# Joined feature sums and a split accumulator bank in the first stage of an attention and mixture kernel

## The chip, the cores and the metric

The kernel runs on one core of one Trainium2 chip. The metric is the device time of one execution in microseconds. The core has TensorE (PE, matrix products; its weight loads are shown as PEld), VectorE (DVE), ScalarE (ACT), GpSimd (POOL) and SyncE (SP, which issues nearly all transfers). TensorE writes its products into accumulator banks, and VectorE and ScalarE read them from there.

## The reference

Three layers follow each other, all in float32. The first is a linear attention with exponential features of both signs:

```python
def phi(x):
    proj = np.einsum('bhsd,df->bhsf', x, w_phi)
    proj = proj - np.max(np.abs(proj), axis=-1, keepdims=True)
    return np.concatenate([np.exp(proj), np.exp(-proj)], axis=-1)
q_p, k_p = (phi(q), phi(k))
kv = np.einsum('bhsf,bhsd->bhfd', k_p, v)
z = np.sum(k_p, axis=2)
num = np.einsum('bhsf,bhfd->bhsd', q_p, kv)
den = np.einsum('bhsf,bhf->bhs', q_p, z)[..., None] + 1e-06
```

There are 4 sequences of 576 tokens, 8 heads of 64 and 128 features of either sign. The second layer normalises each of the 2304 tokens and applies a gated feed-forward (512 to 1536 to 512). The third is a soft mixture of 8 experts with 4 slots each: softmax over tokens into the slots, two products per expert, softmax over slots back to the tokens.

## The kernel before

The work has a first stage (keys and values), a second stage (six blocks of 384 tokens through the gated feed-forward, with the query side of later blocks between) and a last stage (the experts and the output). The change lies in the first.

The first stage goes over 18 tiles of 128 tokens. For a tile, `project` makes the key projections P (L503: sixteen instructions on 64 rows of the array by 128 columns, two products at a time), `shift` takes the largest absolute value and subtracts it on VectorE (L507, L511), `exps` makes both exponentials on ScalarE (L524, L525) into a tile `kp`. Then `kv` adds to three accumulators of the sequence. `kv_of` (L548) multiplies values (64 columns of the array at a time, two products side by side) with the features of one half of the heads, and `z_of` (L557) multiplies a column of ones (32 columns at a time, four side by side), which sums the features. In a trace one product in float32 is two instructions. A sequence ends in the middle of tiles 4 and 13, so these have two parts, and there are 20 parts in all. At the end of a sequence `Evac` copies the accumulators out and `turn` transposes them (kvt, L585).

Between these stand the steps of block 0's query side, class `Rows`: `project` (L389, P from qraw), VectorE's largest and difference (L392, L393), `turn` (L404, T) and ScalarE's exponentials (L406); later `attend` (L449, o), `scale` and `out` (L476, yT). Their place in the code comes from the table `TURNED0`.

The accumulator memory of this stage has three banks for the sums, two for P and three buffers under the tag "misc" for everything else: block 0's P and T, o, yT and kvt. `WARM` products of zeros that nobody reads run at the start while the first transfers are under way (L609).

Each engine executes its instructions in the order of its queue. That order is not the order of the code: a scheduler in the language's layer lays it out when the program is built, by dependencies and its own costs. Semaphores hold an instruction until what it needs has ended.

Of the kernel before, what the change touches and what calls it, by code (L numbers as in the profile page):

```python
# [7 lines left out]
F32 = mybir.dt.float32  # L8
F32R = mybir.dt.float32r
U32 = mybir.dt.uint32  # L10
AF = mybir.ActivationFunctionType
ALU = mybir.AluOpType
# [4 lines left out]
NB, NH, SEQ, HD, DF = 4, 8, 576, 64, 128  # L17
NT, DM, DFF = 2304, 512, 1536
NE, SPE, FE = 8, 4, 1024
NS = NE * SPE  # L20
TILES = NT // 128
BLK = 384
NBLK = NT // BLK
TPB = BLK // 128
# [4 lines left out]
KCONV, MCONV = (3, 2), (2, 2)  # L29
NX = 4  # L30
CFIRST = 7
WARM = 3
NLEFT = 2
ELEFT = 4
CTURN = 4
# [32 lines left out]
def tile_kernel(ctx: ExitStack, tc: tile.TileContext, q2T, qT, kT, v, wbd, wg, wv, wo, rmsg, phi, w1, w2, consts, out):  # L68
    nc = tc.nc
    PE, DVE, ACT, POOL, SP = nc.tensor, nc.vector, nc.scalar, nc.gpsimd, nc.sync  # L70
# [30 lines left out]
    xp = pool(qctx, "xp", side="right")  # L101
# [4 lines left out]
    ident = cst[:, 0:128]  # L106
# [85 lines left out]
    kvt = {}  # L192
    xraw = {}
# [11 lines left out]
    class Q:  # L205
# [3 lines left out]
        def __init__(self, sp, ps, blk, bufs):  # L209
            self.sp, self.ps, self.blk, self.bufs = sp, ps, blk, bufs  # L210
            self.raw, self.x, self.e = {}, {}, {}

        def psum(self, name, shape):
            return self.ps.tile(shape, F32, tag="misc", name=name, bufs=self.bufs["misc"])

        def numerator(self, c, e):
            if c == 0:
# [160 lines left out]
    class Turned(Q):  # L378
# [5 lines left out]
                SP.dma_start(out=self.raw[c], in_=q2T[self.blk, c])  # L384

        def project(self, c, i):
            p = self.psum("P", [128, 2, DF])
            o = p.rearrange("p h f -> p (h f)")
            PE.matmul(out=o, lhsT=self.raw[c][:, 128 * i:128 * i + 128], rhs=wbd_f, start=True, stop=True)  # L389
            mx = self.sp.tile([128, 2, 1], F32, tag="mx", name="qmx", bufs=2)  # L390
            self.pr = self.sp.tile([128, 2, DF], F32, tag="pr", name="qpr", bufs=self.bufs["pr"])
            DVE.tensor_reduce(out=mx, in_=p, axis=AX.X, op=ALU.max, apply_absolute_value=True)  # L392
            DVE.tensor_tensor(out=self.pr, in0=p, in1=mx.to_broadcast([128, 2, DF]), op=ALU.subtract)  # L393
            if i == TPB - 1:
                self.load(c + self.bufs["raw"])
            return self.pr

        def turn(self, c, i, pr):
            if i == 0:
                self.e2 = self.sp.tile([128, 2, 2, BLK], F32, tag="e", name="e2", bufs=self.bufs["e"])  # L400
                self.e[2 * c], self.e[2 * c + 1] = self.e2[:, 0], self.e2[:, 1]
            tp = self.psum("T", [128, 2, 128])
            for h in range(2):
                PE.transpose(out=tp[:, h], in_=pr[:, h], identity=ident)  # L404
            for s in range(2):
                ACT.activation(out=self.e2[:, :, s, 128 * i:128 * i + 128], in_=tp, func=AF.Exp, scale=1.0 - 2.0 * s)  # L406
# [30 lines left out]
    class Rows(Turned):  # L437


        def attend(self, c):  # L440
            if c == 0:
                self.y = self.sp.tile([128, TPB, 4, 2, HD], F32, tag="y", name="y", bufs=1)
            e = [self.e.pop(2 * c), self.e.pop(2 * c + 1)]
            o = self.psum("o", [128, TPB, 2, HD + 1])
            for i in range(TPB):
                for b, r0, r1 in batch_parts(self.blk * TPB + i):
                    for hh in range(2):
                        for s in range(2):
                            PE.matmul(out=o[r0:r1, i, hh], lhsT=e[hh][:, s, 128 * i + r0:128 * i + r1],  # L449
                                      rhs=kvt[b][:, 2 * c + hh, s], start=s == 0, stop=s == 1, skip_group_check=True)  # L450
            rd = self.sp.tile([128, TPB, 2, 1], F32, tag="rd", name="rd", bufs=2)
            DVE.tensor_scalar(out=rd, in0=o[:, :, :, HD:HD + 1], scalar1=1e-6, scalar2=None, op0=ALU.add)
            DVE.reciprocal(out=rd, in_=rd)
            DVE.tensor_tensor(out=self.y[:, :, c], in0=o[:, :, :, 0:HD], in1=rd.to_broadcast([128, TPB, 2, HD]), op=ALU.mult)
            for b, t0, t1 in block_parts(self.blk):
                if c == 3 and self.blk * BLK + t1 == (b + 1) * SEQ and b + 2 < NB:
                    kvt[b + 2] = kvp.tile([128, NH, 2, HD + 1], F32, tag="kv", name=f"kv{b + 2}", bufs=2)
                    SP.dma_start(out=kvt[b + 2].rearrange("p h s d -> p (h s d)"), in_=kv_d[b + 2])

        def scale(self):  # L460
            sq = self.sp.tile([128, 2, 2, BLK], F32, tag="e", name="sq", bufs=self.bufs["e"]).rearrange("p a b t -> p (a b t)")
            ms = self.sp.tile([128, TPB], F32, tag="ms", name="ms", bufs=1)
            rows = [self.y[:, i].rearrange("p c h d -> p (c h d)") for i in range(TPB)]
            for i in range(TPB):
                ACT.activation(out=sq[:, DM * i:DM * i + DM], in_=rows[i], func=AF.Square, accum_out=ms[:, i:i + 1])
            DVE.tensor_scalar(out=ms, in0=ms, scalar1=1.0 / DM, scalar2=1e-6, op0=ALU.mult, op1=ALU.add)
            rsqrt(self.sp, ms)
            for i in range(TPB):
                DVE.tensor_scalar(out=rows[i], in0=rows[i], scalar1=ms[:, i:i + 1], scalar2=None, op0=ALU.mult)

        def out(self):
            xraw[self.blk] = xp.tile([128, 4, BLK], F32, tag="xraw", name="xraw", bufs=1)
            for c in range(4):
                tp = self.psum("yT", [128, TPB, 128])
                for i in range(TPB):
                    PE.transpose(out=tp[:, i], in_=self.y[:, i, c].rearrange("p h d -> p (h d)"), identity=ident)  # L476
                ACT.activation(out=xraw[self.blk][:, c].rearrange("p (i t) -> p i t", i=TPB), in_=tp, func=AF.Copy, scale=rms_sb[:, c:c + 1])

    with ExitStack() as pk:
        kx = pool(pk, "kx")  # L480
        sp = pool(pk, "spk")
        psk = pool(pk, "psk", PSUM)
        acc = {}

        class Front:

# [30 lines left out]
        class K(Front):  # L517
# [2 lines left out]
                SP.dma_start(out=self.vt, in_=v[self.i].rearrange("p (h d) -> p h d", h=NH))  # L520

            def exps(self, hf):
                kp = sp.tile([128, 4, 2, DF], F32, tag="kp", name="kp", bufs=6)
                ACT.activation(out=kp[:, :, 0], in_=self.pr[hf], func=AF.Exp)  # L524
                ACT.activation(out=kp[:, :, 1], in_=self.pr[hf], func=AF.Exp, scale=-1.0)  # L525
                self.e[hf] = kp

            def kv(self, part):

                for f in (self.kv_of, self.z_of):  # L530
                    for hf in range(2):
                        f(hf, part)

            def ends(self, part):
                b, r0, r1 = part
# [25 lines left out]
        class Evac:  # L561
# [17 lines left out]

            def turn(self, n):  # L580
                kv = self.kv
                tp = psk.tile([128, 2, 2, 128], F32, tag="misc", name="kvt", bufs=3)
                for c in range(2):
                    for s in range(2):
                        PE.transpose(out=tp[:, c, s], in_=self.sb[n][:, c, s], identity=ident)  # L585
                for c in range(2):
                    if n < 2:
                        o = kv[:, 4 * c + n:4 * c + n + 3:2, :, 0:HD].rearrange("p h s d -> p s h d")
                        i = tp[:, c].rearrange("p s (h d) -> p s h d", h=2)
                    else:  # L590
                        o = kv[:, c::2, :, HD].rearrange("p h s -> p s h")
                        i = tp[:, c].rearrange("p s (h r) -> p s h r", h=4)[:, :, :, 0]
                    if n == 1:
                        DVE.tensor_copy(o, i)
                    else:
                        ACT.copy(out=o, in_=i)
                if n == 2 and self.b >= 2:
                    SP.dma_start(out=kv_d[self.b], in_=kv.rearrange("p h s d -> p (h s d)"))

        kb = {"tag": "k", "raw": 4, "pr": 3, "P": ("P", 2)}  # L600
        ks = [K(sp, psk, kT, i, kb if i else dict(kb, P=("misc", 3))) for i in range(TILES)]
        ks[0].load(ACT)
        SP.dma_start(out=wbd_f, in_=wbd)
        still = sp.tile([128, 256], F32, tag="kvs0", name="still", bufs=1)
# [20 lines left out]
                k.shift(hf)  # L625
                k.exps(hf)
        fillers = []
        q0 = Rows(sp, psk, 0, {"misc": 3, "raw": 2, "pr": 3, "e": 2})
        qsteps = q0.steps(TURNED0[0:4], TURNED0[4:8], TURNED0[8:])
        qsteps = [[f for m, f in qsteps if m == n] for n in range(2 * TILES)]  # L630
        q0.begin()
        for i in range(TILES):
            k, kn = ks[i], ks[i + 2] if i + 2 < TILES else None
# [85 lines left out]
    with ExitStack() as p2:  # L719
# [5 lines left out]
        sp = pool(tctx, "conv")  # L725
# [233 lines left out]
        t = gate(0, xs)  # L959
# [8 lines left out]
        for blk in range(NBLK):  # L968
            acc = [ps.tile([128, DM], F32, tag=f"acc{i}", name=f"acc{i}", bufs=1) for i in range(TPB)]
            qsteps, qnext = qnext or [], None  # L970
            if blk == 1:
                q1ctx.close()
                sp = pool(pctx, "post", side="right")
            if blk == NBLK - 1:
# [5 lines left out]
                sp = pool(pctx, "post", side="right")  # L980
                hp = pool(pctx, "hp", side="right")
            if blk:
                x2 = []
                for i in range(TPB):
                    y = sp.tile([128, DM], F32, tag="x2", name="x2", bufs=TPB)
# [27 lines left out]
            for m in range(MF):  # L1013
# [3 lines left out]
                if more:  # L1017
                    t = gate((m + 1) % MF, xs)
# [34 lines left out]
    with ExitStack() as p3:  # L1053
        sp = pool(p3, "sp3")
# [145 lines left out]
```

## Time and profile before

| | |
|---|---|
| median of 3 runs | 706.3 us (705.16 to 707.02) |
| profiled execution | 705.7 us, span 703.9 us |
| TensorE busy | 689.4 us, 98% of the span |
| VectorE, ScalarE, GpSimd busy | 468.5, 329.1, 147.2 us |
| first product of the second stage (gate of block 0) | 118.05 us from the span's start |
| transfers | 79.42 MB, mean 113 GB/s |

Times in the rows are microseconds from the start of the span unless marked ns. L12 is line 12 of the kernel before. A timeline row is a run of equal instructions of one engine; its first number is the start and its second the time that the run covers. Products overlap at their ends, so the time from one run's start to the next one's start tells more than the covered time.

### The profile page before, as it was taken

The numbers are of one execution on the slowest core, as the hardware profiler recorded it, in microseconds if no ns is written. First come the engines' busy times: TensorE is split into PE (matmuls) and PEld (weight loads), VectorE is DVE, ScalarE is ACT, GpSimd is POOL, SyncE is SP. The second block draws the span as 40 slices with busy tenths as digits, with TensorE's granted clock in tenths as the row PEclk, the third lists the DMA queues.
The fourth block names the chain that finished last, engine by engine and source line by source line (L and its number), as shares of the span: only waits on it lengthen the run. The fifth ranks groups of instructions, "written<-read, shape, count | busy, mean of one in ns | idle before, by whom it ended". The sixth has DMA issues, their size and how long they took to land.

```text
span 703.9 us, 11807 instructions
## 1 busy us (share of the span) xinstructions
PE 689.4 (98%) x4653; PEld 571.3 (81%) x4653; DVE 468.5 (67%) x915; ACT 329.1 (47%) x687; POOL 147.2 (21%) x74
## 2 busy tenths in 40 slices
PE   7999999999999999999999999999999999999995
PEld 4667766988889898998989989899897999898443
DVE  4798995888875596765857669776585753423313
ACT  4878885687745443344432554425443232112103
POOL 0000000000003355133651326523364200000100
PEclk9999999999999999999999999999999999999997
DMA  6755535434211001010000100001000085577898
GB/s 224 280 170 192 195 107 181 143 120 160 79 40 33 3 24 40 0 57 12 24 9 1 57 13 23 9 0 57 1 1 8 1 305 234 190 284 256 323 367 291
DMA packets 25143, 79.42 MB, mean 113 GB/s; under 512 B 2688, under 2 KB 13376, under 8 KB 18688
## 3 DMA queue, kind: packets, MB, share of 16 engines
q1 hardware_dynamic: 24720, 77.52, 31.4%
q10 hardware_dynamic: 368, 1.15, 0.5%
q8 instruction: 36, 0.59, 0.3%
q14 instruction: 19, 0.16, 0.1%
HBM read 71.99 MB, written 6.67 MB: 112 GB/s over the span
## 4 chain that ended last, share of the span: by engine, by line
PE 96%; DMA 1%; ACT 1%; DVE 1%; issue 0%; SPq 0%; ACTq 0%
PE pg L928 22%; PE pv L928 22%; PE acc L953 7%; PE acc L954 7%; PE acc L955 7%; PE kacc L548 5%; PE num L223 4%; PE P L503 3%; PE kacc L557 3%; PE y L1088 2%; PE y L1072 2%; PE o L449 2%; PE P L389 1%; DMA wraw<-in_wo_dram 1%; PE x2tp L738 1%; PE qP L315 1%
## 5 line engine op out<-in xcount | busy, mean ns | idle before, releaser
L928 PE MATMUL pv<-xnh,wv 128*128 128x384 f32 x576 | 117.1, 343 | 0.0
L928 PE MATMUL pg<-xnh,wg 128*128 128x384 f32 x576 | 115.1, 342 | 0.3 <-ACT xnh L121 0.3
L318 POOL PARTITION_ALL_REDUCE qe<-qe x32 | 51.9, 1634 | 297.1 <-ACT qe L317 287.9
L928 PEld LDWEIGHTS pg<-xnh,wg 128*128 128x128 f32 x576 | 102.5, 188 | 5.8 <-ACT xnh L121 0.7
L928 PEld LDWEIGHTS pv<-xnh,wv 128*128 128x128 f32 x576 | 101.7, 188 | 1.5 <-issue 1.3
L349 POOL PARTITION_ALL_REDUCE qe<-qe x32 | 82.7, 2631 | 85.8 <-DVE qe L348 56.3
L121 ACT CAST hh<-t 128x384 fp32r<-128x384 f32 x72 | 36.7, 509 | 115.2 <-PE acc L954 77.6
L953 PE MATMUL acc<-wo,hh 128*128 128x512 f32 x216 | 87.2, 404 | 0.0
L954 PE MATMUL acc<-wo,hh 128*128 128x512 f32 x216 | 86.1, 399 | 0.0
L955 PE MATMUL acc<-wo,hl 128*128 128x512 f32 x216 | 85.3, 395 | 0.0
L124 DVE TENSOR_TENSOR hl<-t,hh 128x384 fp32r<-128x384 f32 x72 | 40.1, 557 | 63.3 <-ACT hh L121 63.2
L936 DVE SCALAR_TENSOR_TENSOR t<-t,pg 128x384 f32<-128x384 f32 x72 | 39.8, 553 | 57.9 <-ACT t L935 57.7
L935 ACT ACTIVATE t<-pg 128x384 f32<-128x384 f32 x72 | 35.1, 487 | 73.1 <-PE pg L928 72.7
L928 PE MATMUL pg<-xnl,wg 128*128 128x384 f32 x288 | 65.0, 342 | 0.0
L928 PE MATMUL pv<-xnl,wv 128*128 128x384 f32 x288 | 62.4, 339 | 0.0
L940 DVE TENSOR_TENSOR t<-t,pv 128x384 f32<-128x384 f32 x72 | 39.6, 549 | 24.6 <-PE pv L928 23.6
L928 PEld LDWEIGHTS pg<-xnl,wg 128*128 128x128 f32 x288 | 51.9, 188 | 1.6 <-DVE xnl L124 0.9
L928 PEld LDWEIGHTS pv<-xnl,wv 128*128 128x128 f32 x288 | 51.7, 188 | 0.0
L955 PEld LDWEIGHTS acc<-wo,hl 128*128 128x128 f32 x216 | 40.6, 188 | 10.2 <-DVE hl L124 0.3
L953 PEld LDWEIGHTS acc<-wo,hh 128*128 128x128 f32 x216 | 40.8, 189 | 7.3 <-issue 0.3
L954 PEld LDWEIGHTS acc<-wo,hh 128*128 128x128 f32 x216 | 40.6, 188 | 6.3
L548 PE MATMUL kacc<-kp,vt 128*64 128x256 f32 (+1 forms) x320 | 41.2, 393 | 2.3 <-ACT kp L525 2.3
(207 smaller groups left out, 1051.7 us busy)
## 6 DMA issues: line engine op xcount, KB each, us to landing
eu<-in_w_dram SPq DMA_DIRECT2D x32, 1024.0 KB, 6.6
wraw<-in_wg_dram SPq DMA_DIRECT2D x6, 1024.0 KB, 4.9
wraw<-in_wv_dram SPq DMA_DIRECT2D x6, 1024.0 KB, 5.6
wraw<-in_wo_dram SPq DMA_DIRECT2D x6, 1024.0 KB, 5.5
qraw<-in_qT_dram SPq DMA_DIRECT2D x32, 192.0 KB, 2.4
vt<-in_v_dram SPq DMA_DIRECT2D x18, 256.0 KB, 3.2
out_dram<-ob SPq DMA_DIRECT2D x18, 256.0 KB, 3.0
raw<-in_kT_dram SPq DMA_DIRECT2D x17, 256.0 KB, 2.9
```

Source lines behind the costliest of these rows:

```text
L121: ACT.copy(out=hi, in_=src)
L124: (lo_eng or POOL).tensor_tensor(out=lo, in0=src, in1=hi.bitcast(F32), op=ALU.subtract)
L318: POOL.partition_all_reduce(e[:, 0], e[:, 1], channels=128, reduce_op=bass_isa.ReduceOp.absmax)
L349: POOL.partition_all_reduce(e[hh][:, 1], u, channels=128, reduce_op=bass_isa.ReduceOp.add)
L548: PE.matmul(out=kva[o0:o0 + 64, hh // 2], lhsT=self.vt[r0:r1, h], rhs=kp[r0:r1, hh].rearrange("p s f -> p (s f)"), start=first and hh < 2, ...
L928: PE.matmul(out=p, lhsT=w[:, a, c], rhs=x, start=n == 0, stop=n == 11)
L935: ACT.activation(out=t, in_=g, func=AF.Tanh, scale=0.5)
L936: DVE.scalar_tensor_tensor(out=t, in0=t, scalar=1.0, in1=g, op0=ALU.add, op1=ALU.mult)
L940: DVE.tensor_tensor(out=t, in0=t, in1=wide("v", m, xs), op=ALU.mult)
L953: PE.matmul(out=acc[i], lhsT=hh[:, s], rhs=w[:, 0], start=m == 0, stop=False)
L954: PE.matmul(out=acc[i], lhsT=hh[:, s], rhs=w[:, 1], start=False, stop=False)
L955: PE.matmul(out=acc[i], lhsT=hl[:, s], rhs=w[:, 0], start=False, stop=m == MF - 1)
```

## The change

The sums of features of a part are put off: `kv` makes the products kv at once and keeps the part in a list, and when two parts are in it, or the sequence ends, the sums of all of them are made one behind the other. For this `kp` has eight buffers in place of six. The query projections and turns of block 0 no longer take a "misc" buffer but one half of a bank of their own, each call the other half, and "misc" has two buffers in place of three. The result of `attend` goes straight into `xraw`, and `scale` and `out` work on it there, so the tile `y` is gone. There are four unread products at the start in place of three.

```diff
-WARM = 3
+WARM = 4
...
+        def half(self, name):
+
+            if "half" not in self.bufs:
+                return self.psum(name, [128, 2, 128])
+            if not self.halves:
+                t = self.ps.tile([128, 2, 2, 128], F32, tag="halves", name="halves", bufs=1)
+                self.halves = [t[:, 0], t[:, 1]]
+            self.halves.reverse()
+            return self.halves[0]
...
         def project(self, c, i):
-            p = self.psum("P", [128, 2, DF])
+            p = self.half("P")
...
-            tp = self.psum("T", [128, 2, 128])
+            tp = self.half("T")
...
-                self.y = self.sp.tile([128, TPB, 4, 2, HD], F32, tag="y", name="y", bufs=1)
+                xraw[self.blk] = xp.tile([128, 4, BLK], F32, tag="xraw", name="xraw", bufs=1)
...
-            rows = [self.y[:, i].rearrange("p c h d -> p (c h d)") for i in range(TPB)]
+            rows = [xraw[self.blk][:, :, 128 * i:128 * i + 128] for i in range(TPB)]
...
-                kp = sp.tile([128, 4, 2, DF], F32, tag="kp", name="kp", bufs=6)
+                kp = sp.tile([128, 4, 2, DF], F32, tag="kp", name="kp", bufs=8)
...
             def kv(self, part):
 
-                for f in (self.kv_of, self.z_of):
-                    for hf in range(2):
-                        f(hf, part)
+                for hf in range(2):
+                    self.kv_of(hf, part)
+                zs.append((self, part))
+                if len(zs) == 2 or self.ends(part)[1]:
+                    for k, p in zs:
+                        for hf in range(2):
+                            k.z_of(hf, p)
+                    zs.clear()
...
-                tp = psk.tile([128, 2, 2, 128], F32, tag="misc", name="kvt", bufs=3)
+                tp = psk.tile([128, 2, 2, 128], F32, tag="misc", name="kvt", bufs=2)
...
-        ks = [K(sp, psk, kT, i, kb if i else dict(kb, P=("misc", 3))) for i in range(TILES)]
+        ks = [K(sp, psk, kT, i, kb if i else dict(kb, P=("misc", 2))) for i in range(TILES)]
...
-        q0 = Rows(sp, psk, 0, {"misc": 3, "raw": 2, "pr": 3, "e": 2})
+        q0 = Rows(sp, psk, 0, {"misc": 2, "half": True, "raw": 2, "pr": 3, "e": 2})
```

Since the scheduler lays out the queues, the change also moves work that the diff does not touch. Counted in TensorE's order from the first P to the last query projection of the stage, runs of products of one kind go from 23 to 26 for kv (L548, now L563), from 21 to 13 for sums (L557, now L572) and from 17 to 25 for P (L503, now L513). Changes from one kind of product to another, where query projections, turns, kvt, o and yT count as one kind since all use the whole array, go from 76 to 92.

TensorE's order at the start, before. Idle is the unread product, P with raw the key projection, kacc with vt the products kv, kacc with small the sums; a row is a run of equal products.

```order
L609 MATMUL idle<-still 32x256 x3
L503 MATMUL P<-wbd_f,raw 128x128 x16
L548 MATMUL kacc_190<-kp,vt 64x256 x4
L557 MATMUL kacc_192<-kp,small 32x256
L548 MATMUL kacc_191<-kp,vt 64x256
L503 MATMUL P<-wbd_f,raw 128x128 x8
L548 MATMUL kacc_191<-kp,vt 64x256 x3
```

The same place of the changed kernel; halves with qraw is a query projection into the split bank.

```order
L624 MATMUL idle<-still 32x256 x4
L513 MATMUL P<-wbd_f,raw 128x128 x16
L400 MATMUL halves<-wbd_f,qraw 128x256
L563 MATMUL kacc_191<-kp,vt 64x256 x4
L563 MATMUL kacc_192<-kp,vt 64x256
L513 MATMUL P<-wbd_f,raw 128x128 x8
L563 MATMUL kacc_192<-kp,vt 64x256 x3
```

A query projection has moved ahead of the first kv, and the sums of the first part have gone from here.

TensorE's order over tiles 2 and 3, before; T with qpr is a turn of block 0's queries, P with qraw a query projection.

```order
L548 MATMUL kacc_190<-kp,vt 64x256 x4
L548 MATMUL kacc_191<-kp,vt 64x256 x4
L557 MATMUL kacc_192<-kp,small 32x256 x8
L404 MATMUL T<-cst,qpr 128x128 x2
L389 MATMUL P<-wbd_f,qraw 128x256
L404 MATMUL T<-cst,qpr 128x128 x2
L503 MATMUL P<-wbd_f,raw 128x128 x8
L548 MATMUL kacc_190<-kp,vt 64x256 x4
```

The same place of the changed kernel, with what each row waits for: DVE and Activation are VectorE's and ScalarE's semaphores, DMAHW a transfer's.

```order
L415 MATMUL halves<-cst,qpr 128x128 [waits DVE_49]
L415 MATMUL halves<-cst,qpr 128x128
L513 MATMUL P<-wbd_f,raw 128x128 [waits DMAHW6_49,DVE_49,PE_49]
L513 MATMUL P<-wbd_f,raw 128x128 x2
L513 MATMUL P<-wbd_f,raw 128x128 [waits DVE_49,PE_49]
L513 MATMUL P<-wbd_f,raw 128x128 x3
L400 MATMUL halves<-wbd_f,qraw 128x256 [waits Activation_49]
L513 MATMUL P<-wbd_f,raw 128x128
L563 MATMUL kacc_191<-kp,vt 64x256 [waits DMAHW2_49]
L563 MATMUL kacc_191<-kp,vt 64x256 x3
L563 MATMUL kacc_192<-kp,vt 64x256 x4
L572 MATMUL kacc_193<-kp,small 32x256
```

A query projection stands inside a run of key projections, seven before it and one behind; its wait is for ScalarE's exponentials of the turn ahead of it, which read the other half of the bank. The first of sixteen sums stands ahead of the next turn, and fifteen follow it.

## Rows read from the trace of the kernel before

**Rows 1.** The page, busy time with its share, and the chain of waits.

```profile
PE 689.4 (98%) x4653; PEld 571.3 (81%) x4653; DVE 468.5 (67%) x915; ACT 329.1 (47%) x687; POOL 147.2 (21%) x74
...
PE 96%; DMA 1%; ACT 1%; DVE 1%; issue 0%; SPq 0%; ACTq 0%
```

**Rows 2.** Stretches: length, each engine's busy time, granted clock (PEclk), transfer share, GB/s.

```profile
core 0: us, PE busy (x) PEld busy (x) DVE busy (x) ACT busy (x) POOL busy (x), PEclk, DMA share, GB/s
...
9.65:13.03 3.38, 3.38 (x12) 1.00 (x10) 1.59 (x3) 3.01 (x6) 0.00 (x0) 0.50 0.80 299
13.05:118.00 104.95, 103.35 (x1091) 68.49 (x1090) 89.19 (x154) 80.81 (x151) 0.00 (x0) 1.00 0.52 178
...
118.00:703.90 585.90, 576.79 (x3513) 497.94 (x3513) 373.64 (x749) 242.04 (x526) 147.02 (x70) 0.99 0.28 98
```

**Rows 3.** Timeline of TensorE, one tile: start, covered time, line, tiles, shapes, count.

```profile
26.81 1.16 PE L503 MATMUL P<-wbd_f,raw 64*128 64x128 f32 x16
27.90 1.95 PE L548 MATMUL kacc<-kp,vt 128*64 128x256 f32 x16
29.78 1.07 PE L557 MATMUL kacc<-kp,small 128*32 128x256 f32 x16
30.78 0.44 PE L404 MATMUL T<-cst,qpr 128*128 128x128 f32 x2
```

**Rows 4.** Timeline of TensorE, two shorter runs of kv.

```profile
14.31 1.08 PE L548 MATMUL kacc<-kp,vt 128*64 128x256 f32 x6
...
16.32 1.08 PE L548 MATMUL kacc<-kp,vt 128*64 128x256 f32 x8
```

**Rows 5.** Timeline of TensorE, the start; in brackets idle time and its releaser.

```profile
1.18 2.77 PE L609 MATMUL idle<-still 128*32 128x256 f32 x6 [1.18 <-DVE small L606]
4.25 2.97 PE L503 MATMUL P<-wbd_f,raw 64*128 64x128 f32 x32 [0.30 <-DMA raw<-in_kT_dram]
9.48 1.88 PE L548 MATMUL kacc<-kp,vt 128*64 128x256 f32 x8 [2.26 <-ACT kp L525]
```

**Rows 6.** The first transfer of query rows.

```profile
L384 SPq DMA_DIRECT2D qraw<-in_q2T_dram x1: 430/430/430, 5.1 to 5.1; - x1
...
DMA to landing us min/median/max: 5.4/5.4/5.4
```

**Rows 7.** Timeline of all engines around the stall at 40.84 us.

```profile
40.84 0.70 PE L389 MATMUL P<-wbd_f,qraw 128*128 128x256 f32 x2 [1.33 <-ACT kv L596]
41.07 0.41 DVE L393 TENSOR_TENSOR qpr<-P,qmx 128x256 f32<-128x256 f32 x1
```

**Rows 8.** Timeline of TensorE, query projections and turns.

```profile
38.48 0.60 PE L389 MATMUL P<-wbd_f,qraw 128*128 128x256 f32 x2
...
53.61 0.39 PE L404 MATMUL T<-cst,qpr 128*128 128x128 f32 x2
...
61.06 0.65 PE L389 MATMUL P<-wbd_f,qraw 128*128 128x256 f32 x2
61.64 1.16 PE L503 MATMUL P<-wbd_f,raw 64*128 64x128 f32 x16
...
66.31 0.38 PE L404 MATMUL T<-cst,qpr 128*128 128x128 f32 x2
```

**Rows 9.** Timeline of ScalarE, exponentials of two turns.

```profile
54.03 0.66 ACT L406 ACTIVATE e<-T 128x256 f32<-128x256 f32 x2 [0.29 <-PE T L404]
...
68.84 0.67 ACT L406 ACTIVATE e<-T 128x256 f32<-128x256 f32 x2
```

**Rows 10.** Timeline of all engines, the end of the stage.

```profile
115.78 1.53 PE L585 MATMUL kvt<-cst,kvs 128*128 128x128 f32 x12
...
116.48 0.65 ACT L596 COPY kvx<-kvt 128x256 f32<-128x256 f32 x2
...
117.35 0.24 ACT L596 COPY kvx<-kvt 128x8 f32<-128x8 f32 x2 [0.22 <-PE kvt L585]
117.47 1.35 ACT L121 CAST xnh<-xraw 128x384 fp32r<-128x384 f32 x3
...
118.05 0.62 PE L928 MATMUL pg<-xnh,wg 128*128 128x384 f32 x2 [0.30 <-ACT xnh L121]
```

## Prediction before the run

> **What bounds the kernel now.** I read three views in this order: the page's shares with its chain of waits, then busy time by stretch, then the timeline of the first stage. The page is to show that TensorE is busy for 98% of the span and makes 96% of the chain [rows 1]. By stretch, the first stage from 13.05 to 118.00 us has TensorE busy for 103.35 of 104.95 us, VectorE for 89.19 and ScalarE for 80.81 [rows 2]. So what is added to TensorE's work there moves the end by as much, and what VectorE or ScalarE gain is worth nothing unless TensorE waits for it. After 118 us TensorE is busy for 576.79 of 585.90 us in work that the change leaves alone apart from its first few products; I pass a shift of the first stage on to the end one for one.
>
> The timeline of a tile in the steady part gives the prices. From start to start the projections P take 1.09 us, the products kv 1.88, the sums of features 1.00 [rows 3]. A kv run of eight instructions takes 1.08 us and one of sixteen 1.95, so eight more cost 0.87, or 0.109 each [rows 3, 4]. Sixteen at 0.109 are 1.74: a run of kv has a fixed part of 0.14. The sums run four strips at a time, so their sixteen instructions are four rounds of 0.218 and the fixed part is 0.13. P's instructions have half the columns: 16 times 0.054 is 0.87, fixed part 0.22. A query projection of two instructions needs 0.435 and is followed by P after 0.58 [rows 8]: 0.15. On the mean a change from one kind of product to another costs 0.16 us. A second price: six kv instructions (three products) take as long as eight, both 1.08 [rows 4]. A product without a partner in the other strip costs a pair's time: 0.435 for kv, 0.22 for P.
>
> **The change part by part.** *Joined sums.* Eight pairs of runs become one run each. A saved boundary is worth 0.13: 8 x 0.13 = -1.05 us.
>
> *What the order does with the query work.* The counts of runs in TensorE's order go from 23 to 26 for kv, from 17 to 25 for P and from 76 to 92 for all changes of kind. Joining alone would have left 68, so 24 are new: projections and turns of block 0 now stand inside runs (seven P, a query projection, one P; one sum, a turn, fifteen sums). 24 x 0.16 = +3.85. Cut at odd places, five more kv products and three more P products run alone: 5 x 0.435 + 3 x 0.22 = +2.85. No other work covers this, since it is TensorE's own time in a stage in which it is the bound. From both sides: that a P run cut by a query projection pays at its exit is not in the trace, since P is followed by kv everywhere. If all the P cuts were free (8 x 2 x 0.16 and 0.65) the sum would be 3.2 less; if each cut cost twice the dearest fixed part, 24 x 0.44, it would be 6.7 more. I take 0.16, the mean of the four rows.
>
> The Trainium skill ("TensorEngine Tiling (Array Packing)", section "Key Properties") says that changing the tiling mode, not just the tile, drains the engine, and it counts row tiling as a mode. P runs in 64-row tiles and the query work on the whole array, so by that page the unseen exit is paid too and the sum keeps its 3.2; if only the width in columns counted, it would lose it. The seen prices of 0.13 to 0.22 agree with a drain.
>
> *The start.* The fourth unread product has two instructions of 0.43 (six take 2.77, with the last one's end [rows 5]). They end near 4.6 us, the first P waits for its key tile until 4.25: +0.35, but this is covered, because the order now puts the first query projection ahead of the first kv. Its rows of q are issued at 5.1 us and land 5.4 us later [rows 6], at about 10.45. The first kv started at 9.48 [rows 5]; now TensorE stands idle until 10.45, about 1.0 us longer. All behind it, the other kv and the P of tile 2, queues behind this wait, and VectorE and ScalarE have nothing more to do once tiles 0 and 1 are through. From 9.65 to 13.03 the granted clock is 0.50 (1.2 of 2.4 GHz) after the engine's idle time [rows 2], so the time lost there is worth half: 0.14 in full and 0.83 halved make +0.55. Both ends: 0 if the rows land before 9.48; 2.3 if the clock stays at the lower level for another 3.4 us, which costs 1.7.
>
> *The bank in halves.* Before, projections, turns and the rest shared three banks; now the query work has one bank in two halves and the rest two banks. The one stall of the stage, 1.33 us at 40.84, is a query projection that waits for ScalarE to copy a turned kv out of a shared bank [rows 7]. It no longer does: -1.35. But in the new order a projection into the one half waits for ScalarE's exponents out of the other half (order rows with their waits), so the bank is one buffer. A turn's exponents end 1.1 us after its start at the quickest and 3.2 at the slowest (53.61 to 54.69, 66.31 to 69.51) [rows 8, 9]. At six places (four times a turn, 4 to 7 P and a projection; a turn, fifteen sums and a turn; a turn, six of kvt, one P and a turn) TensorE has 0.95 to 1.4 us of work from the turn's start to the next of the two. A projection's release by VectorE took 3.0 us at the pair of kvt (38.48 to 41.48 [rows 7, 8]); there 2.0 us of work now stand between. At 1.1 us per hand-over the seven waits cost 0.3 in all; with 3.2 for the six and 3.0 for the seventh they cost 13 (19.2 less 7.0 of work between, and 1.0). I take 0.2 each, nearer the quick end, as a waiting TensorE lets the other queues run empty: +1.4. What waits behind each is TensorE's whole order.
>
> The Trainium skill ("PSUM — Partial Sum Buffer", section "PSUM bank collisions raise a hardware error") says to guard that memory by bank and quadrant and not by address, since two engines on one bank collide even at other addresses. By it two halves of a bank can't be two buffers, and the 1.4 stay; were they two, the term would be nothing. No run here has shown either yet.
>
> *The end of the stage.* The three turns of the last kv ran in 1.37 us with three buffers [rows 10]. With two the third waits until ScalarE has copied the first (116.48 and 0.65: 117.13). It started near 116.6, so its copy (117.35) and, behind it on ScalarE, the cast that the first gate waits for (117.47, gate at 118.05) come 0.5 later. The gate's first products now have products of val between them while the casts follow at 0.4 us, which gives some 0.2 back: +0.3. Bounds 0 and 0.6.
>
> *At nothing.* y kept in xraw: as many instructions of the same sizes, in a stage where VectorE has 15 us to spare. Eight buffers of kp instead of six: room only. Two banks for tile 0's P instead of three: it has two halves.
>
> The sum: -1.05 + 3.85 + 2.85 + 0.55 - 1.35 + 1.4 + 0.3 = +6.55. The profiled execution took 705.7 us (span 703.9), so 712.25. The median of the runs shown is 706.3, and I lean a little to it: 712.5.
>
> **Rivals.** *The cuts are free.* The query work goes where TensorE has slack between runs and drains cost nothing there. For it: the order was made by something that expects these places to be ready. Against: in the steady part TensorE shows no idle time, every boundary shows its price. It gives -1.05 + 0.55 - 1.35 + 0.3 = -1.55: 704.15 from the profiled execution, 704.75 from the median, not slower. It decides if a new boundary with its lone products costs under 0.06 instead of 0.28 us.
> *Half of it.* Cuts of P by whole-array work cost nothing and nothing waits for the bank: 712.25 - 3.2 - 1.4 = 707.65.
> *The waits rule.* The hand-overs cost 0.6 each (4.2 in place of 1.4) and the longer idle time at the start keeps the clock at 1.2 GHz for another stretch of 3.4 us (+1.7): 716.75. For it: ScalarE and VectorE are busy for 77 and 85% of the stage, and hand-overs of 3 us are in the trace.
>
> **How the numbers follow.** Forecast 0.62, with its own range of 709.5 to 715.5 (half or twice the waits, cuts between 0.10 and 0.22); free cuts 0.11; half of it 0.12; waits 0.15. The range goes from 707, which holds most of the half case, to 717.3. A measurement of this kernel can't tell 0.3% (2.1 us) from no change: under 704.2 is 0.05 (most of free cuts lies just above), 704.2 to 708.4 is 0.06 from free cuts, 0.08 from the half case and 0.01 from the forecast's own tail, 0.15; the rest is slower, 0.80.
>
> **What would show it.** Right: the start of the first gate at 124 to 125 us instead of 118.05; TensorE's first query projection near 10.5, with an idle time of near 2.9 us before it; P runs of sixteen still 1.09 and the cut ones 1.09 and 0.42; sums of 32 instructions in 1.87; no idle time before the projection between the turns of the first kv's parts. Wrong: runs as long as before at every cut (free cuts), or idle times of over 1 us that ScalarE's exponents end (waits), or a granted clock of 0.50 past 13.1 us.

## The result and the profile after

The changed kernel takes 713.5 us in the median of 4 runs (711.4 to 714.7), the kernel before 706.3. The ratio is 1.0106 with an interval of 1.0089 to 1.0122: the change makes the kernel slower by about 7.2 us, and 712.5 had been forecast. The profiled execution has a span of 711.4 us against 703.9.

First the page of the changed kernel: busy time with its share, and the chain of waits. It answers to [rows 1].

```profile
PE 697.7 (98%) x4655; PEld 576.4 (81%) x4655; DVE 469.1 (66%) x915; ACT 329.8 (46%) x687; POOL 147.2 (21%) x74
...
PE 96%; DMA 1%; ACT 1%; DVE 1%; issue 0%; SPq 0%; ACTq 0%
```

TensorE has 8.3 us more of busy time with two instructions more, and bounds the kernel as before. By stretch (the columns of [rows 2]: length, busy time of each engine, granted clock), with the stage cut at the changes of the clock and at the first gate:

```profile
10.31:13.72 3.41, 3.41 (x16) 1.91 (x18) 2.16 (x5) 2.83 (x6) 0.00 (x0) 0.50 0.56 207
13.72:125.75 112.03, 110.85 (x1088) 72.21 (x1085) 89.32 (x153) 81.47 (x151) 0.00 (x0) 1.00 0.49 167
125.75:711.40 585.65, 576.15 (x3513) 497.75 (x3513) 373.33 (x749) 242.09 (x526) 146.99 (x70) 1.00 0.28 98
```

The first gate starts at 125.75 instead of 118.05 us, and what follows takes 585.65 us against 585.90. All of the loss, 7.7 us, lies in the first stage. VectorE's and ScalarE's busy time there is nearly what it was.

Next the timeline of TensorE (start, covered time, line, tiles, shapes, count, in brackets idle time and its releaser): the start, whole runs, and places where the query work stands inside other runs.

```profile
9.60 0.70 PE L400 MATMUL halves<-wbd_f,qraw 128*128 128x256 f32 x2 [1.80 <-DMA qraw<-in_q2T_dram]
10.23 2.78 PE L563 MATMUL kacc<-kp,vt 128*64 128x256 f32 x10
...
21.25 1.16 PE L513 MATMUL P<-wbd_f,raw 64*128 64x128 f32 x16
22.34 1.95 PE L563 MATMUL kacc<-kp,vt 128*64 128x256 f32 x16
...
24.59 1.39 PE L513 MATMUL P<-wbd_f,raw 64*128 64x128 f32 x14
26.18 0.70 PE L400 MATMUL halves<-wbd_f,qraw 128*128 128x256 f32 x2 [0.20 <-ACT e L417]
26.80 0.49 PE L513 MATMUL P<-wbd_f,raw 64*128 64x128 f32 x2
27.22 1.95 PE L563 MATMUL kacc<-kp,vt 128*64 128x256 f32 x16
...
40.97 0.70 PE L400 MATMUL halves<-wbd_f,qraw 128*128 128x256 f32 x2 [0.28 <-DVE qpr L404]
...
57.53 1.93 PE L572 MATMUL kacc<-kp,small 128*32 128x256 f32 x32
59.40 0.70 PE L400 MATMUL halves<-wbd_f,qraw 128*128 128x256 f32 x2
...
62.65 0.71 PE L513 MATMUL P<-wbd_f,raw 64*128 64x128 f32 x8
63.29 0.70 PE L400 MATMUL halves<-wbd_f,qraw 128*128 128x256 f32 x2
63.92 0.71 PE L513 MATMUL P<-wbd_f,raw 64*128 64x128 f32 x8
64.57 1.95 PE L563 MATMUL kacc<-kp,vt 128*64 128x256 f32 x16
...
74.01 0.93 PE L513 MATMUL P<-wbd_f,raw 64*128 64x128 f32 x6
74.87 0.65 PE L563 MATMUL kacc<-kp,vt 128*64 128x256 f32 x2
75.45 1.16 PE L513 MATMUL P<-wbd_f,raw 64*128 64x128 f32 x8
76.53 1.94 PE L563 MATMUL kacc<-kp,vt 128*64 128x256 f32 x14
```

Read starts against starts. A whole P run still takes 1.09 (21.25 to 22.34). Cut after eight, its parts take 0.64 and 0.65 (62.65 and 63.92), 1.29 together, and the query projection between them 0.63 instead of the 0.58 that it has ahead of P in [rows 8]. The stall of 1.33 at 40.84 [rows 7] is gone; 0.28 stands in its place. The two waits for the other half of the bank are 0.20 and 0.28. The sums of two tiles, 32 instructions, take 1.87 instead of twice 1.00.

The end of the stage, timeline of all engines, answers to [rows 10]: the third kvt waits 0.30 for ScalarE's copy of the first, and the chain of copy, cast and gate follows it.

```profile
122.96 1.09 PE L600 MATMUL kvt<-cst,kvs 128*128 128x128 f32 x8
...
124.36 0.66 PE L600 MATMUL kvt<-cst,kvs 128*128 128x128 f32 x4 [0.30 <-ACT kvx L611]
...
125.05 0.24 ACT L611 COPY kvx<-kvt 128x8 f32<-128x8 f32 x2 [0.75 <-PE kvt L600]
125.17 1.76 ACT L121 CAST xnh<-xraw 128x384 fp32r<-128x384 f32 x4
...
125.75 0.62 PE L943 MATMUL pg<-xnh,wg 128*128 128x384 f32 x2 [0.30 <-ACT xnh L121]
```

To see which products pay, I summed over the timeline of each profile, from the first product to the first gate, the time from each product's start to the next one's, by kind of product; idle times over 0.15 us are a column of their own. "Half clock" is the length of the stretches with a granted clock of 0.50 behind the first 9 us; a stretch of 3.4 us at half the clock loses up to 1.7. The last five rows are of experiments told below.

| profile | P | kv | sums | q and T | unread | other | idle | first gate | half clock |
|---|---|---|---|---|---|---|---|---|---|
| before | 20.82 | 39.56 | 21.00 | 10.14 | 2.77 | 18.39 | 4.19 | 118.05 | 3.4 |
| after | 25.64 | 42.23 | 19.73 | 11.97 | 3.55 | 18.58 | 2.87 | 125.75 | 3.4 |
| sums alone | 21.78 | 40.09 | 19.73 | 10.15 | 2.77 | 18.35 | 5.43 | 119.47 | 3.4 |
| halves alone | 23.87 | 43.12 | 20.55 | 11.96 | 2.77 | 18.87 | 3.11 | 125.43 | 0 |
| zsplit | 20.97 | 43.13 | 23.85 | 10.14 | 2.77 | 18.39 | 4.78 | 125.22 | 6.8 |
| unpaired | 32.15 | 38.83 | 20.15 | 10.15 | 2.77 | 18.39 | 2.19 | 125.81 | 0 |
| warm3 | 26.83 | 42.60 | 20.17 | 11.98 | 2.77 | 18.57 | 3.14 | 127.23 | 3.4 |

From before to after P costs 4.82 more, kv 2.67, q and T 1.83; the sums save 1.27 and the idle time 1.32.

### The profile page after: what moved, and what is told of

The parts are those of the page before. It is cut to its first block, busy times and chain, and to the rows that moved or that the text cites. A ratio compares the mean times of both kernels' runs of the same rounds, so it can differ in the third digit from the quotient of the medians.

```text
span 711.4 us, 11786 instructions
## 1 busy us (share of the span) xinstructions
PE 697.7 (98%) x4655; PEld 576.4 (81%) x4655; DVE 469.1 (66%) x915; ACT 329.8 (46%) x687; POOL 147.2 (21%) x74
## 4 chain that ended last, share of the span: by engine, by line
PE 96%; DMA 1%; DVE 1%; ACT 1%; issue 0%; SPq 0%; ACTq 0%; DVEq 0%
PE pg L943 22%; PE pv L943 22%; PE acc L968 7%; PE acc L969 7%; PE acc L970 7%; PE kacc L563 5%; PE num L234 4%; PE kacc L572 3%; PE P L513 3%; PE y L1103 2%; PE y L1087 2%; PE o L460 2%; PE halves L400 1%; PE x2tp L753 1%; PE qP L326 1%; PE qP L325 1%
## 5 line engine op out<-in xcount | busy, mean ns | idle before, releaser
L955 DVE TENSOR_TENSOR t<-t,pv 128x384 f32<-128x384 f32 x72 | 39.5, 549 | 25.2 <-PE pv L943 24.4
L563 PE MATMUL kacc<-kp,vt 128*64 128x256 f32 (+1 forms) x320 | 44.0, 394 | 0.0
```

What stands on the lines that cost most here:

```text
L563: PE.matmul(out=kva[o0:o0 + 64, hh // 2], lhsT=self.vt[r0:r1, h], rhs=kp[r0:r1, hh].rearrange("p s f -> p (s f)"), start=first and hh < 2, ...
L955: DVE.tensor_tensor(out=t, in0=t, in1=wide("v", m, xs), op=ALU.mult)
```

## The experiments

My theory was that the time is lost to runs cut in TensorE's order, that the split bank is what makes the order cut, and that the joined sums are harmless. Rivals were the waits at the bank itself, the changed start, and the joined sums.

**One part alone.** *sums* has the joined sums, the eight buffers of kp and y in xraw, but the three shared buffers and three unread products. Against the changed kernel:

```diff
-WARM = 4
+WARM = 3
...
-                tp = psk.tile([128, 2, 2, 128], F32, tag="misc", name="kvt", bufs=2)
+                tp = psk.tile([128, 2, 2, 128], F32, tag="misc", name="kvt", bufs=3)
...
-        q0 = Rows(sp, psk, 0, {"misc": 2, "half": True, "raw": 2, "pr": 3, "e": 2})
+        q0 = Rows(sp, psk, 0, {"misc": 3, "raw": 2, "pr": 3, "e": 2})
```

> The change without the bank in halves and without the fourth unread product: sums joined, y in xraw, three shared buffers. By the theory that the order's cuts cost the time (0.16 us for each change of kind, a pair's time for a lone product): 69 changes of kind in place of 76 and one more lone kv, so 705 to 706.5 us, the time of before or a little under. By the rival that putting the sums off costs it (features are held longer, the sums come late): 711 to 714 us, as the whole change.

Measured: ratio 1.0031 (1.0015 to 1.0047), 706.8 against 705.3 us, a little above the 705 to 706.5 that had been expected. TensorE's order has 69 changes of kind (76 before). The sums give back their 1.27, but the query projection at the pair of kvt now comes earlier and waits longer for ScalarE, and a stretch at half the clock follows it. Timeline of TensorE and, behind it, busy time by stretch (the columns of [rows 2]):

```profile
39.96 0.70 PE L400 MATMUL P<-wbd_f,qraw 128*128 128x256 f32 x2 [3.06 <-ACT kv L611]
40.59 1.16 PE L513 MATMUL P<-wbd_f,raw 64*128 64x128 f32 x12
41.68 3.35 PE L563 MATMUL kacc<-kp,vt 128*64 128x256 f32 x16
```

```profile
41.16:44.57 3.41, 3.41 (x22) 2.01 (x20) 2.79 (x5) 1.14 (x2) 0.00 (x0) 0.50 0.27 82
```

A run of sixteen kv takes 3.35 us there instead of 1.95. The joined sums can't be the cause of 7 us.

*halves* has the split bank and its two shared buffers (with the eight buffers of kp and y in xraw too), without the joined sums and with three unread products:

```diff
-WARM = 4
+WARM = 3
...
-                for hf in range(2):
-                    self.kv_of(hf, part)
-                zs.append((self, part))
...
+                for f in (self.kv_of, self.z_of):
+                    for hf in range(2):
+                        f(hf, part)
```

> The change without the joined sums and with three unread products: the bank in halves and two shared buffers alone. By the theory of the cuts: 105 changes of kind in place of 76 and nine more lone products, +8.9 us by the prices in the trace, less the stall of 1.3 us that goes, plus 0.8 us of waits: 713.5 to 716 us. By the rival that the joined sums cost the time: 705 to 707 us.

Measured: ratio 1.0115 (1.0092 to 1.0138), 712.7 us. This one part makes the whole loss; the time is just under the 713.5 to 716 that had been expected, and the 0.8 us of waits in that sum did not come. Its order has 105 changes of kind, 29 more than before, and its table row shows where they are paid: kv +3.56, P +3.05, q and T +1.82, with 1.1 us less of idle time. Its profile has no stretch at half the clock where the one before has one, so the cuts alone cost up to 1.7 us more than the 7.4 by which the gate is later. The executions agree: four of its five have a mean granted clock of 0.996 to 0.998 and take 712.7 us in the mean, and the eight of 17 of the kernel before with 0.996 or 0.997 take 703.9. TensorE has no wait for the bank over 0.15 us; it pays where the order is cut.

*halves* holds two things, the split bank and two shared buffers in place of three, and they were not run apart. What stands in the cuts speaks for the split bank: of the seven runs of P that it has more than the kernel before, six are made by a query projection and one by a turn, the work that uses the halves, and none by work in a shared buffer.

**Why the order is cut.** The scheduler lays out the queue. *pinned* is the whole change, with TensorE's instructions of the first stage held to the order of the code (each step's products are tied behind those of the step before by dependencies that set only the order); *sums_pinned* holds the same order without the split bank, that is with *sums*' three shared buffers. Both orders have 62 changes of kind.

```diff
-                k.kv(parts[0])
+                placed(lambda: k.kv(parts[0]), PE.engine)
...
-                kn.project()
+                placed(kn.project, PE.engine)
...
-                    fillers.pop(0)()
+                    placed(fillers.pop(0), PE.engine)
```

> The whole change with TensorE's order of the first stage held to the order of the code: no run is cut (62 changes of kind), and the turns and projections into the two halves stand side by side. If the cuts alone cost the time, and halves of a bank are free: 703 to 705 us. If the bank is one buffer, the cuts turn into waits: about six times turn, projection, turn with 0.3 to 0.45 us of work between and 1.1 to 2.5 us until the bank is read, and some five more pairs: 710 to 718 us, with idle time on TensorE that ScalarE's exponents and VectorE's differences end.

> The same held order with three shared buffers in place of the bank in halves and with three unread products: it differs from the held change in the banks and one unread product alone. By the theory of cuts and one buffer: no cuts and few waits, 2.9 us less than before by the counts: 702 to 705 us. If the order costs nothing and something else of the change does (sums put off, y in xraw): 710 to 714 us.

Measured: *pinned* 735.4 us, ratio 1.0419 (1.0394 to 1.0444), far above the 710 to 718 expected if the bank is one buffer; *sums_pinned* 710.9, ratio 1.0084 (1.006 to 1.0108). The waits of *pinned* in the first stage (engine, line, releaser: us in total, times, longest), TensorE's own:

```profile
PE halves L400 <- ACT e L417: 7.7, 4, 2.9
...
PE halves L400 <- DVE qpr L404: 5.7, 3, 3.4
...
PE halves L415 <- DVE qpr L404: 4.9, 4, 2.0
...
PE P L513 <- issue: 3.5, 1, 3.5
```

and two places of its timeline:

```profile
30.39 1.22 PE L400 MATMUL halves<-wbd_f,qraw 128*128 128x256 f32 x2 [2.87 <-ACT e L417]
32.59 0.69 PE L415 MATMUL halves<-cst,qpr 128*128 128x128 f32 x2 [0.98 <-DVE qpr L404]
33.20 2.08 PE L513 MATMUL P<-wbd_f,raw 64*128 64x128 f32 x16
```

A projection (L400) waits for ScalarE's exponentials of a turn (L417), which read the other half. With the products side by side as the code has them, TensorE waits 18.3 us for hand-overs of the bank, and the clock is at 0.50 behind the longest (the P run of sixteen at 33.20 takes 2.08). Over the 148.12 us of its first stage the granted clock is 0.90 in the mean, some 30 us at 0.50, which the expectation had left out. In *sums_pinned*, at the same order with three buffers, none of these waits is left:

```profile
PE P L513 <- DVE pr L521: 4.6, 4, 3.5
PE P L513 <- issue: 1.5, 1, 1.5
...
PE P L400 <- ACT kv L611: 0.8, 1, 0.8
```

So the two halves are one buffer, and as such they cost 24.5 us at this order (735.4 less 710.9, the clock's stretches among it); with the order cut the same bank costs the 7 us of *halves*. That the scheduler moves the query work apart because of these waits is argued from the pair of runs; its choice itself was not traced and is not shown. The Trainium skill ("PSUM — Partial Sum Buffer", section "PSUM bank collisions raise a hardware error") says to guard accumulator memory by bank and quadrant, not by address; the waits of *pinned*, 18.3 us for a half while the other half is in use, agree with it.

*sums_pinned* was a miss: I expected a gain. With P of the third tile held ahead of the first kv, TensorE stands 3.52 us until 9.99 waiting for VectorE's differences, and two stretches at half the clock follow. Held order is no gain by itself.

```profile
9.99 0.46 PE L513 MATMUL P<-wbd_f,raw 64*128 64x128 f32 x2 [3.52 <-DVE pr L521]
```

**What a change of kind costs.** *zsplit* is the kernel before with kv and sums alternating by half of the heads. Its order has 114 changes of kind instead of 76, with the same products.

```diff
-                for f in (self.kv_of, self.z_of):
-                    for hf in range(2):
+                for hf in range(2):
+                    for f in (self.kv_of, self.z_of):
                         f(hf, part)
```

> The kernel before with the products kv and the sums taken in turns by half of the heads (kv, sums, kv, sums for each part): the same products, no bank changed, TensorE's order has 114 changes of kind in place of 76. If a change costs what the trace of before shows (0.13 to 0.16 us): +5 to +6 us, near 711. If a change of kind costs nothing and the lone products or the waits alone made the time: +0 to +1 us.

Measured: 713.4 us against 704.2, ratio 1.0133 (1.0115 to 1.0151), more than 38 changes account for. TensorE's timeline in a steady tile and, behind it, where a second stretch at half the clock lies (43.53 to 46.94):

```profile
27.99 1.08 PE L548 MATMUL kacc<-kp,vt 128*64 128x256 f32 x8
29.00 0.64 PE L557 MATMUL kacc<-kp,small 128*32 128x256 f32 x8
29.57 1.08 PE L548 MATMUL kacc<-kp,vt 128*64 128x256 f32 x8
30.59 0.64 PE L557 MATMUL kacc<-kp,small 128*32 128x256 f32 x8
31.16 0.44 PE L404 MATMUL T<-cst,qpr 128*128 128x128 f32 x2
...
42.47 0.70 PE L389 MATMUL P<-wbd_f,qraw 128*128 128x256 f32 x2 [2.02 <-ACT kv L596]
43.10 1.72 PE L503 MATMUL P<-wbd_f,raw 64*128 64x128 f32 x16
44.74 1.97 PE L548 MATMUL kacc<-kp,vt 128*64 128x256 f32 x8
46.65 0.76 PE L557 MATMUL kacc<-kp,small 128*32 128x256 f32 x8
47.34 1.08 PE L548 MATMUL kacc<-kp,vt 128*64 128x256 f32 x8
```

From 27.99 to 31.16 are 3.17 us against 2.88 in [rows 3]: two more changes, 0.145 each. Over the stage kv and sums cost 6.4 us more (the table). Of these 1.0 lies in the second stretch at half the clock, where eight kv take 1.91 instead of 1.01 and eight sums 0.69 instead of 0.57; what is left, 5.4, is 0.14 for each of 38. The rest of the 7.2 by which the gate is later is the stall ahead of that stretch, grown from 1.33 to 2.02. So this change of kind costs 0.14, as the fixed parts of kv (0.14) and of the sums (0.13) have it; the forecast's 0.16 was a mean over four kinds. The Trainium skill ("TensorEngine Tiling (Array Packing)", section "Key Properties") says that a change of tiling mode drains the engine; here it is between 64 and 32 columns, and the price agrees with a drain.

**What a lone product costs.** *unpaired* is the kernel before with the four P products of one half of the rows issued first and then the four of the other half, where they alternate before.

```diff
-                for c in range(4):
-                    for hf in range(2):
+                for hf in range(2):
+                    for c in range(4):
```

> The kernel before, with one thing changed: a tile's eight key projections P are issued as four on the one half of the array's rows and then four on the other, where they alternate before. The counts of runs stay nearly as they are (78 changes of kind against 76), the buffers too. It tells apart two readings of the P pieces, which cost 4.8 us more in the changed kernel where 2.4 were forecast. Theory (a P product that has no partner in the other row strip takes a pair's time): a run of sixteen has about seven rounds instead of four, so 16 instructions cost about 1.09 + 3 or 4 x 0.22 = 1.75 to 1.95 us from start to start; over 18 tiles +12 to +16 us, 717 to 721 us against about 705. Rival (the partner does not matter, a P piece costs by its cuts alone): a run of sixteen still takes 1.1 us, and the time is 704 to 707.

Measured: 714.1 and 715.5 us in two executions against 705.5, 1.3% slower; two others took 725.3 and 726.6, which makes the median 720.4 and the ratio over all four 1.0212 (1.0129 to 1.0294). The profile is of the first, and what the last two lost beyond it is not known. TensorE's timeline:

```profile
27.10 1.71 PE L503 MATMUL P<-wbd_f,raw 64*128 64x128 f32 x16
28.74 1.95 PE L548 MATMUL kacc<-kp,vt 128*64 128x256 f32 x16
```

The same sixteen instructions take 1.64 instead of 1.09 us (1.75 to 1.95 had been expected), and P costs 11.3 us more in the stage. The halves of the rows work side by side where products for both stand close together in the queue; in runs of four and four most of that is lost.

With this the P column can nearly be worked out from the order alone. Written as the half of the rows that each product uses, a tile's P reads 01010101 in nearly all of the kernel before (four rounds). In the changed kernel there are pieces such as these:

```
0101.0101   00011.101   0.000.1111   00.0111.01   0001110.1
```

A dot is a cut; a product whose neighbour is on the same half needs a round of its own. The profile does not print the halves, but the pieces' times bear such strings out: the three products on one half at 74.01 take 0.86 (three rounds and a fixed part make 0.88), the four at 75.45 take 1.08 (1.10). Counted through, with 0.22 us for a round and 0.22 for a piece's fixed part (the prediction's own two prices):

| kernel | pieces | rounds | worked out | measured |
|---|---|---|---|---|
| before | 17 | 77 | 20.7 | 20.82 |
| after | 25 | 86 | 24.4 | 25.64 |
| halves | 24 | 86 | 24.2 | 23.87 |
| unpaired | 19 | 127 | 32.1 | 32.15 |
| warm3 | 26 | 90 | 25.5 | 26.83 |

Three of the five come within 0.4 us and two are 1.2 to 1.3 low. The close fit of *unpaired* is in part luck: seven rounds and a fixed part make 1.76 for each of its fourteen steady runs, which take 1.64, and its first runs take as much more than the count leaves for them.

**The start.** *warm3* is the whole change with three unread products. The first query projection then stays behind the first kv, and the order has 97 changes of kind.

```diff
-WARM = 4
+WARM = 3
```

> The whole change with three unread first products instead of four. The scheduler then leaves the first query projection behind the first kv, and TensorE's order has 97 changes of kind instead of 92. Theory (the time goes with the cuts; the fourth product and the early query projection are worth next to nothing): +5 x 0.17 to 0.28 for the cuts, about -0.5 at the start: 713 to 715 us, within 0.3% of the whole change's 713.5. Rival (the early query projection, its wait for the query rows at the start and the stretch at half the clock behind it are a main part of the loss): 709 to 711.5 us.

Measured: 713.6 us, ratio 1.0114 (1.0093 to 1.0135): as slow as the whole change, so the fourth product and the early query projection are not where the 7 us go; its five changes of kind more, 0.8 us at 0.16, could hide a loss of that size. TensorE's timeline has the first kv at its old place again:

```profile
9.48 1.24 PE L563 MATMUL kacc<-kp,vt 128*64 128x256 f32 x8 [1.95 <-ACT kp L535]
```

**Looking for a gain.** The stall that grew in *sums* hangs on the place of one query step, so *sums_q9* and *sums_q10* put that step later, and *sums_q10w4* has the fourth unread product too.

```diff
-TURNED0 = [2, 8, 14, 20, 12, 15, 20, 26, 28, 33]
+TURNED0 = [2, 10, 14, 20, 12, 15, 20, 26, 28, 33]
```

> Joined sums with three shared buffers and three unread products, and the second group of query projections one step later, away from the turns of the first kv: 66 changes of kind in place of 76, no lone product more than before. By the counts 1.4 us under before, and 1.3 us less if the stall between the turns of the first kv goes too: 703 to 705.5 us against 705.3 to 706.3 of before. If putting the sums off has a cost of its own: 706 to 708 us.

> The same with that group two steps later: 68 changes of kind, the turns of the first kv finished before the projections need a shared buffer. By the counts 1.1 us under before and the stall surely gone: 703 to 705 us. If putting the sums off has a cost of its own: 706 to 708 us.

> The kernel with that group two steps later, and four unread products in place of three: the order then has the first query projection ahead of the first kv, as in the whole change, and is else nearly the same (67 changes of kind). If the wait for the query rows costs as predicted: 0.3 to 1 us more than the same kernel with three. If the longer warm-up pays by the clock: up to 1.7 us less.

Measured against 704.2 us: 705.1, ratio 1.0009 (0.9993 to 1.0024); 704.1, ratio 0.9994 (0.9981 to 1.0007); 703.8, ratio 0.9997 (0.9981 to 1.0013). The step to 10 takes the loss of *sums* away, and the fourth product adds nothing that can be measured, but none of the three is faster than before. The times lie in or near the ranges expected, but the gains of 1.1 us and more behind those ranges do not show, since the kernel before itself ran at 704.2 there. In *sums_q10* the gate stands at 115.40 us and 0.88 of a new stall at 50.09 is left; its profile has no stretch at half the clock, which makes up to 1.7 of the 2.65 us to the kernel before.

## Why the prediction was right

*What bounds the stage* held: TensorE, with the stage's growth of 7.7 us passed on (span +7.5). The first gate was forecast at 124 to 125 and came at 125.75, 0.75 past it.

*Joined sums*, forecast -1.05: the sums' own time fell by 1.27.

*Cuts and lone products*, forecast +6.70 (3.85 and 2.85): P, kv, q, T and the other products of the table cost 9.5 us more. By kind the forecast was 2.66 for kv (three more runs at 0.16, five lone products at 0.435), measured 2.67; 2.1 for the other thirteen changes, measured 2.0. P is the term that was mis-sized: eight pieces at 0.16 and three lone products at 0.22 make 1.94, measured 4.82. The step that failed is "three more P products run alone": I counted pieces with an odd number of products, one lone product in each. An odd piece can lie on one half altogether (the six instructions at 74.01, three products, take 0.86), and an even piece can be unpaired as well (the eight at 75.45 take 1.08, as long as sixteen). By halves of the rows there are nine more rounds, not three, and a piece's fixed part for P is 0.22, not the mean of 0.16: 17 x 0.22 = 3.7. The remaining 1.1 is not fully told: some 0.4 of it is the part of P that lies in the stretch at half the clock (12.95 to 13.72), and the rest stays open.

*The exits of cut P runs*, costed at 0.16 though no row had shown one: paid. The query projection between P at 63.29 takes 0.63, its two instructions 0.435 of it. "The cuts are free" and "half of it" are thereby refuted, and *halves* refutes them by the total.

*The start*, forecast +0.55 with the query rows at 10.45 and 2.9 us of idle time: the rows came in 4.6 us instead of 5.4 and the idle time was 1.80. First kv at 10.23, so +0.75 with the projection ahead of it; the clock's stretch kept its length. The sign and the size were right, the path was not. *warm3*, which has the old start, is no faster: its order has five changes of kind more.

*The stall*, forecast -1.35: gone, as *halves* and after show.

*Bank hand-overs*, forecast +1.4 for seven: two waits, 0.48 us in all. That the bank is one buffer was right. I had taken the quick hand-over as near the mean and added 0.2 each for doubt; in this order nearly all were ready. Of "the waits rule" nothing is seen in the changed kernel; *pinned* is the order in which it rules.

*The end of the stage*, forecast +0.3: the third kvt waited 0.30, and from the first kvt to the gate it is 2.79 us (122.96 to 125.75) instead of 2.27 (115.78 to 118.05), +0.52 as worked out for the gate. Of the 0.2 that was to come back behind the gate, the 0.25 by which that part is shorter may be the sign; a single profile of each can't show it.

The sum came near because two errors were opposed: P cost 2.9 more than I said, idle time and the start together 1.4 less, the sums 0.2 less. That much of the closeness is luck.

## What to carry to other kernels

A buffer that engines hand to each other should have a bank of its own: two halves of a bank are one buffer, and where a scheduler lays out the queue the price may appear not as waits but as products moved into other runs. Where small tiles share the array, count an order by rounds: write down the part of the array that each product uses, since a product without a neighbour on another part takes a pair's time and each cut a fixed part of its own (0.14 to 0.22 us here). An engine at 98% pays for both in full, so look at the order's runs before the waits.

## What was not expected

The stretch at half the clock does not follow from the kernel alone. Before, TensorE idles 2.26 us until 9.48 and the clock is 0.50 from 9.62 to 13.03; in *sums_q10w4* it idles 2.51 until 9.78 and the clock stays. Busy time by stretch there, and the row of the timeline:

```profile
9.78:13.50 3.72, 3.72 (x34) 2.44 (x36) 2.72 (x6) 2.94 (x6) 0.00 (x0) 1.00 0.67 247
```

```profile
9.78 0.70 PE L400 MATMUL P<-wbd_f,qraw 128*128 128x256 f32 x2 [2.51 <-DMA qraw<-in_q2T_dram]
```

The profiles of *halves*, *sums_q10* and *unpaired* have none either, after 2.26 us of idle time in the first two. Each such stretch is worth up to 1.7 us, as much as the smaller effects here, so a gate time of a single profile can be off by that. Executions of one kernel differ in the same way: of the 29 of the kernel before that were taken beside *zsplit*, fourteen have a mean granted clock of 0.997 and take 703.5 us in the mean, ten have 0.994 or 0.995 and take 705.6. What decides it stays open.
